# An attention and mixture-of-experts kernel: expert choice in eight operations a slot, three experts measured during attention, and scaling on ScalarE

## The chip, the cores and the metric

The kernel runs on one core of a Trainium2 chip. The metric is the time of one execution in microseconds on the device, as the median of several runs; smaller is better. One more execution was taken with the hardware profiler, and every row below comes from it. The engines are named as in the profile: PE is the matrix engine (PEld its weight loads), DVE is VectorE, ACT is ScalarE, POOL is GpSimd, SP is SyncE, which issues most of the DMAs.

## The reference

Attention over 8 batches and 8 heads of 576 tokens with 64 features, in which scores that lie more than `tau` below the row's maximum are dropped; its output, rearranged to 4608 rows of 512, goes through a mixture of 8 experts of which each row takes one. Everything is float32.

```python
scores = scale * np.matmul(q, k.transpose(0, 1, 3, 2))
thresh = np.max(scores, axis=-1, keepdims=True) - tau
scores = np.where(scores >= thresh, scores, -1000000000.0)
...softmax, then out = attn @ v
x = attn_out.transpose(0, 2, 1, 3).reshape(4608, 512)
logits = x @ w_gate                       # 512 x 8
e_idx = np.argmax(logits, axis=1)
gate_w = softmax(logits)[row, e_idx]
eom = sigmoid(x @ w_output_gate)
for e in range(8):
    mask = e_idx == e
    h = np.maximum(x[mask] @ w1[e], 0.0)  # 512 x 1024
    out[mask] = gate_w[mask, None] * eom[mask, e, None] * (h @ w2[e])
```

How many rows each expert gets is known only when the kernel runs.

## The kernel before

**Attention** takes about half of the span. It runs in 16 blocks of 9 steps, each block one pair of heads and batches, about 28 us long. PE computes scores, DVE reduces and thresholds them (L159, L189), ACT takes the exponential (L177), PE transposes and multiplies by the values, POOL normalises rows (L324, L325). As soon as rows of x are complete, they are routed: logits, the expert's number, and the place in the expert's list (`place`, L673), after which POOL's indirect DMA scatters the row into a table `xs` in DRAM, sorted by expert.

**Experts.** After attention come 13 units of work, numbered 0 to 12. Units 0 to 2 are early: they take the first 366, 256 and 424 rows of experts 0, 1 and 2, which are there before attention ends. Units 3 to 12 stand for the ten entries of `SLOTS`, taken in the order of `UNITS`; a slot is a number of rows, and which expert it serves is chosen at run time. A unit gathers its rows (`xg`, or `xgn` where it has 256), scales each row to a power of two (`even`, L928), transposes it and splits it in two fp16 halves xh and xl (`prep`), and then goes through 8 columns f: `first(f)` multiplies by 128 hidden features in 12 matmuls (xh, xl with w1h, w1l; L1260), ACT takes the relu and its high half (hr L1262, hh L969), DVE the low half (hl L975), and `second` follows two columns later (L1282 to L1285). Outputs `yo` are scaled by row (L956 on ACT, L958 on DVE) and scattered by POOL (L959).

**Weights** come in chunks of two columns, four chunks an expert, and are split in fp16 halves too: the high ones on ACT (w1h, w2h: L971), the low ones on DVE (w1l, w2l: L977). Before an expert's split its largest weight must be known: `measure` reduces each chunk (L874 on DVE, L875 on ACT), `peak` joins four chunks (L885, L886), `top` is a PE transpose of the result (L891) with a reduction and a diagonal behind it (L896, L897), and `spread` a PE matmul (L903) from which `powers` makes the scale. `SCALE` gives for a unit the column of peak, top and spread. PE takes its instructions in order, so the transpose of `top` stands in the row of matmuls and waits there for DVE.

Experts 0 and 1 (`FIRST = 2`) are measured during attention, in steps of blocks 1, 2, 3, 4, 6, 8, 12 and 15; all others in the expert stage, four columns or more after their load (`weigh`). Weights and rows of a unit can only be loaded once its slot has an expert (`known`).

**Choice.** `choose` fills the ten slots one after the other on DVE, on rows of 8 numbers, in 11 operations a slot; `aside` advances it between columns. For each slot it takes the expert with the most rows left whose remainder is not over the slot, and subtracts. `finish` then totals what is left over, in `sums` and `table` (on rows of up to 352 numbers), for a last loop (`rest`) which runs a whole extra unit for each leftover piece; `total` is the number of its passes.

Two order rules matter for the change. In the loop over columns (`run`) each column issues its matmuls first, then what else belongs to it, and each engine takes its own instructions in that order. And buffers: `egn` holds one gathered 256-row unit, and `eraw1`, the raw weights' second ring, is opened before the pools `ew1` to `ew3` of split weights.

Of the kernel before, what the change touches and what calls it, by code (L numbers as in the profile page):

```python
# [17 lines left out]
P = 128  # L18
# [412 lines left out]
class Router:  # L431
    SLOTS = (420, 396, 512, 504, 496, 256, 256, 256, 256, 256)
# [255 lines left out]

    def choose(self):
        V, E, row, dummy = self.nc.vector, self.E, self.row, self.dummy  # L690
        key, cand, mx, cm, got = row(E, "key"), row(E, "cand"), row(1, "mx"), row(1, "cm"), row(2, "got")
        st = self.st = self.sm.tile([1, 4, E], F32, name="st")
        pick = self.sm.tile([1, 2, E], F32, name="pick")
        V.tensor_tensor(st[:, 0], self.cnt[0:1], self.first[0:1], op=ALU.subtract)
# [53 lines left out]
    def sums(self, c, n):  # L748
        V = self.nc.vector
        V.memset(c[:, 0:1], 0.0)  # L750
        for e in range(self.E):
            V.tensor_tensor(c[:, e + 1 : e + 2], c[:, e : e + 1], n[:, e : e + 1], op=ALU.add)
            if e % 3 == 2:
                yield "vector"

    def table(self, sm, tag, out, c, size, first):
        V, E, NS = self.nc.vector, self.E, out.shape[2]
# [11 lines left out]
        V.tensor_tensor(ina, ina, inb, op=ALU.mult)  # L769
        yield "vector"  # L770
        V.tensor_scalar(v1, c[:, 0:E], -float(size), -dummy, op0=ALU.mult, op1=ALU.add)
        V.tensor_tensor(v1, v1, first, op=ALU.add)
        V.tensor_tensor(inb, ina, be(v1), op=ALU.mult)
        yield "vector"
        V.tensor_reduce(slf[:, 1], inb, axis=AX.X, op=ALU.add)
        V.tensor_reduce(slf[:, 2], ina, axis=AX.X, op=ALU.add)
        yield "vector"
        V.tensor_tensor(inb, ina, be(self.asc[0:1]), op=ALU.mult)
        V.tensor_reduce(slf[:, 0], inb, axis=AX.X, op=ALU.add)
        V.tensor_tensor(slf[:, 2], slf[:, 2], sid, op=ALU.mult)  # L780
        yield "vector"
        V.tensor_scalar(slf[:, 2], slf[:, 2], float(size), dummy, op0=ALU.mult, op1=ALU.add)
        V.tensor_tensor(slf[:, 1], slf[:, 1], slf[:, 2], op=ALU.add)
        V.tensor_copy(out, slf[:, 0:2])


class Experts:
    RINGS, NW, YB = (4, 4), 4, 4
    UNITS = (0, 6, 2, 7, 3, 8, 1, 5, 9, 4)
    TURN = (2,)  # L790
    FIRST = 2
    LOOK = 4
    SCALE = {2: (2, 4, 5), 3: (0, 1, 2), 4: (0, 1, 4)}

    def __init__(self, ctx, tc, rt, ident, w1, w2, out):
# [10 lines left out]
        self.gp, self.gn = [self.pool("eg", 1)], self.pool("egn", 1)  # L806
# [9 lines left out]
    def open(self):  # L816
# [17 lines left out]
        self.wp += [top(f"ew{i}", 1) for i in range(1, self.NW)]  # L834
# [81 lines left out]
    def even(self, xg):  # L916
# [72 lines left out]
    def begin(self):  # L989
# [9 lines left out]
        self.lines = [([n for n, t in enumerate(tiles) if t > 2], 2), ([n for n, t in enumerate(tiles) if t == 2], 1)]  # L999
        self.at, self.since, self.wide, self.pieces = {2: 1, 1: 1}, {1: -self.LOOK}, 0, []  # L1000
# [15 lines left out]
    def gather_next(self, i, f):  # L1016
        rt = self.rt
        passed = i + (f > 6)
        for line, room in self.lines:
            while self.at[room] < len(line):  # L1020
                k = self.at[room]
# [5 lines left out]
                self.at[room] += 1  # L1027
# [3 lines left out]
    def level(self, i, k):  # L1031
        for n in sorted(self.since):
            if self.column - self.since[n] >= self.LOOK or n == i + 1 and k >= -4:
# [81 lines left out]
    def run(self):  # L1115
# [4 lines left out]
        for i in range(nun):  # L1120
            b, final = self.unit(i), i == nun - 1
            late = i == rt.early - 1
            for f in range(8):
# [10 lines left out]
                if len(back) > 2:  # L1134
# [17 lines left out]
                rt.aside(2 if i else 1 if rt.tables else 4)  # L1152
# [32 lines left out]
class Base:  # L1185
# [24 lines left out]
    def even(self):  # L1210
        self.down, pieces = self.ex.even(self.xg[:, 0 : self.nt])
# [126 lines left out]
class Turned(Pair):  # L1338
# [148 lines left out]
def build(tc, qkv, tau, wg, w1, w2, out, shape):  # L1487
    nc = tc.nc
    with ExitStack() as ctx:
# [6 lines left out]
        with tc.manual_schedule(engines=ENGINES):  # L1496
            with ExitStack() as actx:
# [6 lines left out]
                load, size = ((0, 4), (0, 7), (1, 4), (1, 7), (2, 4), (4, 4), (4, 7), (6, 4)), (1, 2, 3, 4, 6, 8, 12, 15)  # L1504
# [24 lines left out]
                def second():  # L1529
# [4 lines left out]
                    ex.unit(0).key()  # L1534

                def first():
# [3 lines left out]
                    ws[2]()  # L1540
                    ws[3]()
# [58 lines left out]
```

## Time and profile before

| | us |
|---|---|
| median of 3 runs | 917.07 |
| the 3 runs | 915.4, 917.07, 917.15 |
| profiled execution | 915.95 |
| its span in the trace | 914.2 |
| attention, with its tail | 0 to about 472 |
| experts | about 462 to 915 |

The two stages overlap by some ten microseconds. The share of an engine's busy time is a mean over both; what a change in one stage is worth is read from that stage. In the views by window, PEclk is the clock that PE was granted: 1.00 is 2.4 GHz and 0.50 is 1.2 GHz.

### The profile page before, as it was taken

To read this page: it belongs to the slowest core of one execution; us is meant where nothing else is said; L and a number is where in the kernel's file an instruction comes from. 1 tells how busy PE (TensorE), PEld (TensorE's weight loads), DVE (VectorE), ACT (ScalarE), POOL (GpSimd) and SP (SyncE) were. 2 spreads that over 40 slices of the span, in tenths; PEclk is the share of its full clock that TensorE was granted. 3 is DMA by queue.
4 is the path that set the end of the run, shared out by engine and by line. 5 is a ranking of instruction groups with operands and counts; after the bars stand their busy time and mean duration, and the time that the engine had idled before them with its cause. 6 is when DMAs were issued, how large, how long until landed. Compare 5 with 4: busy or idle time off the path is not lost. (4 is left out here: it accounts for less than half of the span.)

```text
span 914.2 us, 22624 instructions
## 1 busy us (share of the span) xinstructions
PE 875.4 (96%) x8369; PEld 534.8 (59%) x8369; DVE 795.8 (87%) x1941; ACT 708.8 (78%) x1367; POOL 389.9 (43%) x660
## 2 busy tenths in 40 slices
PE   8999999999999999999988689899999999999996
PEld 4666666666666666666644444456546546566643
DVE  7999999999999999999977999988977877878731
ACT  6999999999989989898875665567857757867731
POOL 4465655757857678578735601021103103102101
PEclk9999999999999999999999999999999999999999
DMA  6499633143421234213259857445645636642001
GB/s 215 160 294 316 196 118 126 48 132 97 135 84 45 85 96 137 85 44 124 82 159 303 240 182 251 141 131 176 208 138 194 219 117 207 184 151 93 24 22 46
DMA packets 73810, 132.73 MB, mean 145 GB/s; under 512 B 6664, under 2 KB 35592, under 8 KB 73697
## 3 DMA queue, kind: packets, MB, share of 16 engines
q1 hardware_dynamic: 67153, 111.10, 38.8%
q0 software_dynamic: 6544, 20.16, 5.8%
q8 instruction: 67, 1.10, 0.5%
q14 instruction: 46, 0.38, 0.1%
HBM read 99.46 MB, written 32.74 MB: 145 GB/s over the span
## 5 line engine op out<-in xcount | busy, mean ns | idle before, releaser
L177 ACT ACTIVATE p<-s,mn 128x576 f32<-128x576 f32 x288 | 215.4, 796 | 22.6 <-DVE s L159 20.4
L189 DVE SCALAR_TENSOR_TENSOR p<-s,thr,p 128x576 f32<-128x576 f32 x288 | 225.9, 821 | 0.7 <-ACT p L177 0.3
L159 DVE TENSOR_SCALAR_CACHE_REDUCE s<-ps 128x576 f32<-128x576 f32 x288 | 206.2, 751 | 13.7 <-PE ps L145 11.1
L959 POOL DMA_INDIRECT out_dram<-yo,kid x39 | 49.7, 1274 | 330.9 <-DVE yo L958 234.7
L145 PE MATMUL ps<-qk 64*128 64x288 f32 (+1 forms) x1280 | 181.1, 418 | 0.0
L166 POOL TENSOR_SCALAR thr<-mn,tau_sb 128x2 f32<-128x2 f32 x144 | 103.3, 718 | 129.7 <-DVE s L159 125.8
L1260 PE MATMUL ph<-xh,w1l 128*128 128x256 f16 (+7 forms) x412 | 130.7, 319 | 1.9 <-DVE w1l L977 1.9
L1260 PE MATMUL ph<-xh,w1h 128*128 128x256 f16 (+7 forms) x412 | 131.6, 320 | 0.7 <-ACT w1h L971 0.7
L1260 PE MATMUL ph<-xl,w1h 128*128 128x256 f16 (+7 forms) x412 | 129.5, 319 | 2.4 <-DVE xl L975 2.4
L145 PEld LDWEIGHTS ps<-qk 64*128 64x128 f32 (+1 forms) x1280 | 107.2, 177 | 17.5 <-DVE s L159 2.5
L1262 ACT ACTIVATE hr<-ph 128x256 f32<-128x256 f32 (+7 forms) x103 | 48.0, 466 | 89.3 <-PE ph L1260 82.2
L1260 PEld LDWEIGHTS <-w1h 128*128 128x128 f16 x832 | 80.7, 99 | 56.9 <-issue 5.2
L258 PE MATMUL pr<-PTb,vld 128*64 128x320 f32 (+1 forms) x640 | 107.2, 447 | 0.0
L975 DVE TENSOR_TENSOR hl<-hr,hh 128x256 f16<-128x256 f32 (+7 forms) x103 | 54.3, 527 | 59.7 <-ACT hh L969 56.8
L244 PE MATMUL pt<-ident,p 64*128 64x64 f32 x2288 | 95.6, 223 | 1.5 <-ACT PTb L250 1.1
L258 PE MATMUL pa<-PTa,vld 128*64 128x256 f32 (+1 forms) x640 | 84.6, 391 | 0.3 <-ACT PTb L218 0.3
L244 PEld LDWEIGHTS pt<-ident,p 64*128 64x128 f32 x2288 | 82.9, 139 | 2.5 <-ACT PTb L250 1.4
L1282 PE MATMUL py<-w2h,hh 128*128 128x512 f16 (+3 forms) x213 | 82.0, 385 | 0.6 <-ACT yo L956 0.6
L1283 PE MATMUL py<-w2l,hh 128*128 128x512 f16 (+3 forms) x213 | 81.7, 384 | 0.0
L247 ACT COPY PTa<-pt 128x1024 f32<-128x1024 f32 x64 | 67.1, 1048 | 0.2 <-PE pt L244 0.2
L324 POOL TENSOR_TENSOR rows<-xl,rinv 128x256 f32<-128x256 f32 x64 | 62.1, 971 | 11.3 <-ACT xl L369 11.0
L247 ACT COPY PTb<-pt 128x1024 f32<-128x1024 f32 x63 | 65.1, 1034 | 1.2 <-PE ps L145 1.1
(244 smaller groups left out, 1707.4 us busy)
## 6 DMA issues: line engine op xcount, KB each, us to landing
r<-in_moe_w_dram SPq DMA_DIRECT2D x112, 512.0 KB
qk<-in_qkv_dram SPq DMA_DIRECT2D x31, 608.0 KB
xs<-zrow SPq DMA_DIRECT2D x44, 257.0 KB
vld<-in_qkv_dram SPq DMA_DIRECT2D x32, 320.0 KB
xg<-xs SPq DMA_DIRECT2D x4, 771.0 KB
xgn<-xs SPq DMA_DIRECT2D x6, 514.0 KB
xg<-xs SPq DMA_DIRECT2D x3, 1028.0 KB
xg<-xs SPq DMA_DIRECT2D x6, 128.5 KB
```

The costliest lines, as they stand in the source:

```text
L145: nc.tensor.matmul(ps[a][rows, o : o + HS], q[pp, t * P : t * P + w], k[pp, k0 : k0 + HS], start=True, stop=True)
L159: nc.vector.tensor_scalar(s, ps[a][:, c0 : c0 + S], SC, None, op0=ALU.mult, op1=ALU.min, accum_out=mn[:, a : a + 1])
L166: self.router.gate = nc.gpsimd.tensor_scalar(thr, mn, self.tau, None, op0=ALU.add)
L177: self.nc.scalar.activation(e, ss[a], AF.Exp, bias=mn[:, a : a + 1], scale=-1.0)
L189: nc.vector.scalar_tensor_tensor(e, s, thr[:, a : a + 1], e, op0=ALU.is_le, op1=ALU.mult, accum_out=acc[:, a ^ (t > 1) : (a ^ (t > 1)) + 1])
L244: nc.tensor.transpose(pt[:, o : o + 64], p[hs[h], k0 : k0 + P], id_[hs[h], hs[h]])
L247: nc.scalar.copy(d, pt.rearrange("p (h b j) -> p b h j", h=2, j=64))
L258: one = lambda out, l, r, start, stop: nc.tensor.matmul(out, l, r, start=start, stop=stop, skip_group_check=True)
L324: nc.gpsimd.tensor_tensor(o, xl[:, a, 0:4, 0:D], ra[:, a, 0:4, None].broadcast_to([P, 4, D]), op=ALU.mult)
L1260: nc.tensor.matmul(ph, w[:, c, fs], x[:, c, 0:N], start=(i == 0), stop=(i == 11))
L1282: nc.tensor.matmul(Y, hh[:, ts], wh, start=(f == 0), stop=False)
L1283: nc.tensor.matmul(Y, hh[:, ts], wl, start=False, stop=False)
```

## The change

The diff has ten parts.

1. `SLOTS` is put in another order (the 396 goes from second to sixth place) and `UNITS` with it. Each unit keeps its number of rows, but unit 4 now takes slot 1, where before it took slot 6.
2. `choose` needs 8 operations a slot, with the tie broken by a fraction added once to the counts, and stops at two places a slot instead of three. `aside` runs two pieces a column until three slots are filled, and then one a column from unit 2 on.
3. `sums` and `table` go from DVE to POOL; the reductions over 8 numbers become three additions of halves (`halved`).
4. `FIRST = 3`: expert 2's four chunks are loaded and measured during attention. Measures now stand in blocks 1, 2, 3, 4, 5, 6, 8, 9, 10, 12, 13 and 15 (5, 9, 10 and 13 are new).
5. The row scaling of units 1 to 5 is done by ACT.
6. `SCALE` holds units 3 and 4 alone: peak in column 3, top in 4, spread in 5 for unit 3, and 2, 4, 5 for unit 4. `weigh` starts at unit 2 for unit 3's chunks.
7. `egn` gets two buffers, so that 256-row units are gathered two ahead.
8. The pool `ew1` is opened before `eraw1`.
9. At the start, unit 0's second(0) comes before first(2), the splits of chunk 0's w2 come earlier, and the last `place` matmul comes a column later.
10. `key` runs at the second half of `prep`.

```diff
-    SLOTS = (420, 396, 512, 504, 496, 256, 256, 256, 256, 256)
+    SLOTS = (420, 256, 512, 504, 496, 396, 256, 256, 256, 256)
...
     def choose(self):
...
+        V.tensor_scalar(part, self.desc[0:1], 1.0 / (4 * E), None, op0=ALU.mult)
+        V.tensor_tensor(st[:, 0], st[:, 0], part, op=ALU.add)
...
         for k, z in enumerate(self.SLOTS):
             yield
-            V.scalar_tensor_tensor(key, st[:, 1], float(read), st[:, 0], op0=ALU.is_ge, op1=ALU.mult)
-            V.tensor_reduce(mx, key, axis=AX.X, op=ALU.max)
-            V.scalar_tensor_tensor(cand, key, mx, self.desc[0:1], op0=ALU.is_equal, op1=ALU.mult)
-            V.tensor_reduce(cm, cand, axis=AX.X, op=ALU.max)
+            V.scalar_tensor_tensor(key[:, 0:E], st[:, 1], float(read), st[:, 0], op0=ALU.is_ge, op1=ALU.mult)
+            V.tensor_reduce(top, key, axis=AX.X, op=ALU.max)
+            V.tensor_scalar(cand, key[:, 0:E], top, None, op0=ALU.is_equal)
+            V.tensor_tensor(pick, st[:, 2:4], cand[:, None, :].broadcast_to([1, 2, E]), op=ALU.mult)
             yield
-            V.tensor_scalar(key, key, 0.0, None, op0=ALU.is_gt)
-            V.scalar_tensor_tensor(cand, cand, cm, key, op0=ALU.is_equal, op1=ALU.mult)
-            V.tensor_tensor(pick, st[:, 2:4], cand[:, None, :].broadcast_to([1, 2, E]), op=ALU.mult)
             V.tensor_reduce(got, pick, axis=AX.X, op=ALU.add)
-            yield
...
     def table(self, sm, tag, out, c, size, first):
-        V.tensor_tensor(ina, bsl(sid), be(c[:, 0:E]), op=ALU.is_ge)
-        V.tensor_tensor(inb, bsl(sid), be(c[:, 1:]), op=ALU.is_lt)
+        for t, edge, op in ((ina, c[:, 0:E], ALU.is_ge), (inb, c[:, 1:], ALU.is_lt)):
+            G.tensor_tensor(t, bsl(sid), be(edge), op=ALU.subtract)
+            G.tensor_scalar(t, t, 0.0, None, op0=op)
...
-    UNITS = (0, 6, 2, 7, 3, 8, 1, 5, 9, 4)
+    UNITS = (0, 1, 2, 6, 3, 7, 5, 8, 9, 4)
-    FIRST = 2
+    FIRST = 3
-    SCALE = {2: (2, 4, 5), 3: (0, 1, 2), 4: (0, 1, 4)}
+    SCALE = {3: (3, 4, 5), 4: (2, 4, 5)}
...
-        self.gp, self.gn = [self.pool("eg", 1)], self.pool("egn", 1)
+        self.gp, self.gn = [self.pool("eg", 1)], self.pool("egn", 2)
...
+        self.wp.append(top("ew1", 1))
         self.raw.append(top("eraw1", self.RINGS[1]))
...
         def scale(a, b):
             for t in range(a, b):
-                V.tensor_scalar(xg[:, t, 0:DM], xg[:, t, 0:DM], up[:, t : t + 1], None, op0=ALU.mult)
+                if other:
+                    self.nc.scalar.activation(xg[:, t, 0:DM], xg[:, t, 0:DM], AF.Copy, scale=up[:, t : t + 1])
+                else:
+                    V.tensor_scalar(xg[:, t, 0:DM], xg[:, t, 0:DM], up[:, t : t + 1], None, op0=ALU.mult)
...
     def look(self, i, f):
-            if age >= self.LOOK:
+            n = self.fresh[0][0] // 4
+            if age >= self.LOOK and (i > 1 or n > 3) and (n == i + 1 or self.column % 2 == 0):
                 self.weigh()
...
     def run(self):
-                if len(back) > 2:
+                if len(back) > (1 if i == 0 and f == 1 else 2):
...
                 if rt.pending is not None:
+                    if rt.ripe:
+                        rt.place(self.ps_x.tile([P, 512], F32, name="px")[:, 0:144])()
                     rt.ripe = True
-                    rt.place(self.ps_x.tile([P, 512], F32, name="px")[:, 0:144])()
...
-                rt.aside(2 if i else 1 if rt.tables else 4)
+                rt.aside(2 if len(rt.tables) < 3 else int(i > 1))
...
-                load, size = ((0, 4), (0, 7), (1, 4), (1, 7), (2, 4), (4, 4), (4, 7), (6, 4)), (1, 2, 3, 4, 6, 8, 12, 15)
+                size = 1, 2, 3, 4, 5, 6, 8, 9, 10, 12, 13, 15
+                load = (0, 4), (0, 7), (1, 4), (1, 7), (2, 4), (2, 7), (4, 4), (4, 7), (5, 4), (6, 4), (8, 4), (9, 4)
```

On DVE, before, in unit 1, this is the stretch that ends in the peak of unit 2 (r_... are raw weights, st, key and cand are `choose`'s, hl and w1l belong to the columns):

```order
L977 SCALAR_TENSOR_TENSOR w2l<-r_8574,upe,w2h 128x1024
L874 TENSOR_REDUCE mx<-r_8819 128x1
L711 TENSOR_SCALAR picks<-got 1x1
L712 CAST picks<-got 1x1
L713 SCALAR_TENSOR_TENSOR st<-cand,st 1x24
L701 SCALAR_TENSOR_TENSOR key<-st 1x8
L702 TENSOR_REDUCE mx<-key 1x1
L703 SCALAR_TENSOR_TENSOR cand<-key,mx,desc 1x8
L704 TENSOR_REDUCE cm<-cand 1x1
L975 TENSOR_TENSOR hl<-hr,hh 128x256
L977 SCALAR_TENSOR_TENSOR w1l<-r_8668,upe,w1h 128x1024
L874 TENSOR_REDUCE mx<-r_8849 128x1
```

The rows after these are the peak, L885 and L886. The same columns of unit 1 in the changed kernel have neither a measure nor a step of the choice between the halves (w2l is L987 here, hl L985):

```order
L987 SCALAR_TENSOR_TENSOR w2l<-r_8611,upe,w2h 128x1024
L985 TENSOR_TENSOR hl<-hr,hh 128x256
L987 SCALAR_TENSOR_TENSOR w1l<-r_8687,upe,w1h 128x1024
L985 TENSOR_TENSOR hl<-hr,hh 128x256
L987 SCALAR_TENSOR_TENSOR w2l<-r_8688,upe,w2h 128x1024
L985 TENSOR_TENSOR hl<-hr,hh 128x256
L987 SCALAR_TENSOR_TENSOR w1l<-r_8707,upe,w1h 128x1024
```

Measures and choice have moved to unit 2, on the same engine. There the peak of unit 3 (L892, L893) stands one column ahead of the reduction that follows its transpose (L903):

```order
L985 TENSOR_TENSOR hl<-hr,hh 128x424
L881 TENSOR_REDUCE mx<-r_9144 128x1
L892 TENSOR_REDUCE red<-mx 128x2
L893 TENSOR_SCALAR red<-red 128x2
L712 SCALAR_TENSOR_TENSOR key<-st 1x8
L713 TENSOR_REDUCE top<-key 1x1
L714 TENSOR_SCALAR cand<-key,top 1x8
L715 TENSOR_TENSOR pick<-st,cand 1x16
L985 TENSOR_TENSOR hl<-hr,hh 128x424
L903 TENSOR_REDUCE most<-px 2x1
```

By `SCALE`, unit 3's peak closes column 3 and its transpose follows the matmuls of column 4; in the kernel before the peak of unit 2 closed column 2 of unit 1, two columns ahead, and that of unit 3 column 0 of unit 2, one column ahead.

On ACT, before, these are the rows at the start of the expert stage, from unit 0's first relu (h0r) to its second (hr):

```order
L1262 ACTIVATE h0r<-ps 128x366
L969 CAST h0h<-h0r 128x366
L971 ACTIVATE w2h<-r_1425,upe 128x1024
L369 COPY xl<-pa 128x400
L369 COPY xl<-pr 128x400
L971 ACTIVATE w1h<-r_2421,upe 128x1024
L971 ACTIVATE w2h<-r_2422,upe 128x1024
L971 ACTIVATE w1h<-r_2597,upe 128x1024
L1262 ACTIVATE hr<-ph 128x366
```

In the changed kernel they read:

```order
L981 ACTIVATE w2h<-r_2948,upe 128x1024
L277 COPY X_223<-pa 128x320
...
L1274 ACTIVATE h0r<-ps 128x366
L979 CAST h0h<-h0r 128x366
L369 COPY xl<-pa 128x400
L369 COPY xl<-pr 128x400
L981 ACTIVATE w1h<-r_3460,upe 128x1024
L981 ACTIVATE w2h<-r_3461,upe 128x1024
L981 ACTIVATE w1h<-r_4471,upe 128x1024
L1274 ACTIVATE hr<-ph 128x366
```

Chunk 0's w2h has moved ahead of h0r. Three splits still stand ahead of hr: those of chunk 1 and the first of chunk 2.

## Rows read from the trace of the kernel before

**Rows 1.** The page's first part: busy time, share of the span, instructions.
```profile
PE 875.4 (96%) x8369; PEld 534.8 (59%) x8369; DVE 795.8 (87%) x1941; ACT 708.8 (78%) x1367; POOL 389.9 (43%) x660
```
**Rows 2.** PE's waits from 462 to 915: total us, times, longest.
```profile
PE px L891 <- DVE red L886: 7.6, 2, 4.5
PE px L891 <- DVE red L885: 6.0, 1, 6.0
PE px L673 <- DVE ohb L588: 3.1, 1, 3.1
PE ph L1260 <- DVE xl L975: 2.4, 2, 1.2
PE px L1236 <- issue: 2.0, 1, 2.0
PE ph L1260 <- DVE w1l L977: 1.9, 1, 1.9
PE py L1285 <- DVE hl L975: 0.8, 1, 0.8
PE ph L1260 <- ACT w1h L971: 0.7, 1, 0.7
```
**Rows 3.** Windows in which PE's clock was halved (columns in the first line).
```profile
core 0: us, PE busy (x) PEld busy (x) DVE busy (x) ACT busy (x) POOL busy (x), PEclk, DMA share, GB/s
...
475.70:478.40 2.70, 2.66 (x9) 1.34 (x10) 1.27 (x2) 2.46 (x3) 0.41 (x2) 0.50 1.04 375
524.50:529.60 5.10, 5.04 (x18) 2.64 (x19) 4.74 (x20) 0.00 (x0) 3.04 (x4) 0.50 1.04 313
550.20:553.50 3.30, 3.30 (x9) 1.31 (x10) 3.13 (x12) 0.34 (x1) 0.00 (x0) 0.50 0.94 343
591.60:594.40 2.80, 2.75 (x9) 1.28 (x10) 2.35 (x8) 0.00 (x0) 0.00 (x0) 0.50 0.54 182
833.40:836.80 3.40, 3.40 (x25) 2.29 (x22) 2.32 (x4) 2.28 (x4) 0.00 (x0) 0.50 0.03 7
```
**Rows 4.** The same view of units 1 to 3 and of the seven units behind.
```profile
500.00:592.00 92.00, 74.08 (x449) 41.30 (x448) 87.62 (x241) 57.60 (x104) 22.79 (x21) 0.94 0.65 201
592.00:820.00 228.00, 227.99 (x1430) 129.95 (x1428) 185.19 (x303) 161.81 (x267) 33.78 (x29) 0.99 0.53 174
```
**Rows 5.** DVE from 500 to 592 by line: count, busy, mean ns, idle before.
```profile
L874 DVE TENSOR_REDUCE mx<-r 128x1 f32<-128x1024 f32 x13 | 15.7, 1204 | 0.0
L928 DVE TENSOR_SCALAR xg<-xg,xup 128x512 f32<-128x512 f32 x10 | 4.4, 478 | 0.0
L707 DVE SCALAR_TENSOR_TENSOR cand<-cand,cm,key 1x8 f32<-1x8 f32 x9 | 1.9, 215 | 0.3
L768 DVE TENSOR_TENSOR inbs<-sid,ci 1x352 f32<-1x352 f32 x1 | 0.5, 506 | 0.0
```
**Rows 6.** ACT from 470 to 910 by line.
```profile
L956 ACT ACTIVATE yo<-py,ksc 128x512 f32<-128x512 f32 x11 | 7.4, 686 | 14.9 <-PE py L1285 14.9
```
**Rows 7.** ACT's timeline at the start: start, us, instruction, idle before.
```profile
475.94 1.15 ACT L971 ACTIVATE w2h<-r,upe 128x1024 f16<-128x1024 f32 x1 [2.69 <-POOL rows L325]
```
**Rows 8.** Windows of three attention blocks, columns as in rows 3.
```profile
31.00:59.00 28.00, 28.00 (x364) 18.34 (x366) 27.44 (x76) 26.64 (x57) 16.17 (x29) 1.00 0.77 232
143.00:171.80 28.80, 28.80 (x368) 18.93 (x367) 28.50 (x84) 26.27 (x57) 18.98 (x40) 1.00 0.29 97
285.40:313.40 28.00, 28.00 (x364) 18.33 (x362) 26.98 (x80) 25.58 (x55) 17.49 (x28) 1.00 0.22 69
```
**Rows 9.** POOL from 100 to 460 by line.
```profile
L324 POOL TENSOR_TENSOR rows<-xl,rinv 128x256 f32<-128x256 f32 x50 | 48.8, 975 | 0.3
```
**Rows 10.** DVE's timeline at the end of attention, two rows of one line.
```profile
464.14 0.37 DVE L338 TENSOR_TENSOR LX<-LX,part 128x160 f32<-128x160 f32 x1
...
473.44 1.04 DVE L338 TENSOR_TENSOR LX<-LX,part 128x160 f32<-128x160 f32 x1
```
**Rows 11.** POOL's timeline at the second of these.
```profile
473.22 0.51 POOL L325 TENSOR_SCALAR rows<-xl,rinv 64x64 f32<-64x64 f32 x1
473.69 0.61 POOL L324 TENSOR_TENSOR rows<-xl,rinv 128x256 f32<-128x256 f32 x1
```

More of the change, by code (lines that the diff above doesn't have):

```diff
@@ L687, in open, with halved @@
         self.chosen = False
+    def halved(self, t, op):
+        n = self.E // 2
+        while n:
+            self.nc.gpsimd.tensor_tensor(t[..., 0:n], t[..., 0:n], t[..., n : 2 * n], op=op)
+            n //= 2
+        return t[..., 0]
     def choose(self):
         V, E, row, dummy = self.nc.vector, self.E, self.row, self.dummy
-        key, cand, mx, cm, got = row(E, "key"), row(E, "cand"), row(1, "mx"), row(1, "cm"), row(2, "got")
+        key, top, cand, got = row(E + 1, "key"), row(1, "top"), row(E, "cand"), row(2, "got")
         st = self.st = self.sm.tile([1, 4, E], F32, name="st")
         pick = self.sm.tile([1, 2, E], F32, name="pick")
+        part = row(E, "part")
+        V.memset(key[:, E:], 0.75)
         V.tensor_tensor(st[:, 0], self.cnt[0:1], self.first[0:1], op=ALU.subtract)
         V.tensor_scalar(st[:, 1], st[:, 0], float(P), float(self.SAFE), op0=ALU.add, op1=ALU.max)
+        V.tensor_scalar(part, self.desc[0:1], 1.0 / (4 * E), None, op0=ALU.mult)
+        V.tensor_tensor(st[:, 0], st[:, 0], part, op=ALU.add)
         V.tensor_scalar(st[:, 2], self.first[0:1], -1.0, dummy, op0=ALU.mult, op1=ALU.add)
@@ L756, in table @@
     def table(self, sm, tag, out, c, size, first):
-        V, E, NS = self.nc.vector, self.E, out.shape[2]
+        G, E, NS = self.nc.gpsimd, self.E, out.shape[2]
         sh = [1, NS, E]
@@ L766, in table @@
         dummy = float(E * self.CAP)
[L767 to L769 removed]
+        for t, edge, op in ((ina, c[:, 0:E], ALU.is_ge), (inb, c[:, 1:], ALU.is_lt)):
+            G.tensor_tensor(t, bsl(sid), be(edge), op=ALU.subtract)
+            G.tensor_scalar(t, t, 0.0, None, op0=op)
+        G.tensor_tensor(ina, ina, inb, op=ALU.mult)
         yield "vector"
[L771 to L773 removed]
+        G.tensor_scalar(v1, c[:, 0:E], -float(size), -dummy, op0=ALU.mult, op1=ALU.add)
+        G.tensor_tensor(v1, v1, first, op=ALU.add)
+        G.tensor_tensor(inb, ina, be(v1), op=ALU.mult)
+        G.tensor_copy(slf[:, 1], self.halved(inb, ALU.add))
         yield "vector"
[L775 to L776 removed]
+        G.tensor_tensor(inb, ina, be(self.asc[0:1]), op=ALU.mult)
+        G.tensor_copy(slf[:, 0], self.halved(inb, ALU.add))
         yield "vector"
[L778 to L784, printed above, removed]
+        G.tensor_tensor(slf[:, 2], self.halved(ina, ALU.add), sid, op=ALU.mult)
+        G.tensor_scalar(slf[:, 2], slf[:, 2], float(size), dummy, op0=ALU.mult, op1=ALU.add)
+        G.tensor_tensor(slf[:, 1], slf[:, 1], slf[:, 2], op=ALU.add)
+        G.tensor_copy(out, slf[:, 0:2])
 class Experts:
     RINGS, NW, YB = (4, 4), 4, 4
[L789 removed]
+    UNITS = (0, 1, 2, 6, 3, 7, 5, 8, 9, 4)
     TURN = (2,)
[L791 removed]
+    FIRST = 3
     LOOK = 4
[L793 removed]
+    SCALE = {3: (3, 4, 5), 4: (2, 4, 5)}
     def __init__(self, ctx, tc, rt, ident, w1, w2, out):
@@ L833, in open @@
         self.load_next()
-        self.wp += [top(f"ew{i}", 1) for i in range(1, self.NW)]
+        self.wp += [top(f"ew{i}", 1) for i in range(2, self.NW)]
     def load(self, e, g, gate=None, k=0):
@@ L914, in spread, with even @@
         return out
-    def even(self, xg):
+    def even(self, xg, other=False):
         V, n, DM = self.nc.vector, xg.shape[1], self.rt.DM
@@ L998, in begin @@
         tiles = [-(-(rt.base[n] if n < rt.early else rt.SLOTS[self.UNITS[n - rt.early]]) // P) for n in range(len(make))]
-        self.lines = [([n for n, t in enumerate(tiles) if t > 2], 2), ([n for n, t in enumerate(tiles) if t == 2], 1)]
-        self.at, self.since, self.wide, self.pieces = {2: 1, 1: 1}, {1: -self.LOOK}, 0, []
+        self.lines = [([n for n, t in enumerate(tiles) if t > 2], 2), ([n for n, t in enumerate(tiles) if t == 2], 2)]
+        self.at, self.since, self.wide, self.pieces = [1, 1], {1: -self.LOOK}, 0, []
         self.first_raws, self.column, self.fresh, self.mx, self.diag = [], 0, [], {}, None
@@ L1018, in gather_next @@
         passed = i + (f > 6)
-        for line, room in self.lines:
-            while self.at[room] < len(line):
-                k = self.at[room]
+        for c, (line, room) in enumerate(self.lines):
+            while self.at[c] < len(line):
+                k = self.at[c]
                 if k >= room and line[k - room] > passed:
@@ L1032, in level @@
         for n in sorted(self.since):
-            if self.column - self.since[n] >= self.LOOK or n == i + 1 and k >= -4:
+            if self.column - self.since[n] >= self.LOOK and (n < i + 3 or i > 4) or n == i + 1 and k >= -4:
                 del self.since[n]
@@ L1210, in even @@
     def even(self):
-        self.down, pieces = self.ex.even(self.xg[:, 0 : self.nt])
+        self.down, pieces = self.ex.even(self.xg[:, 0 : self.nt], 0 < self.i < 6)
         return pieces
@@ L1219, in prep @@
         ex, nc, rt, nt = self.ex, self.nc, self.ex.rt, self.nt
+        if k == 1 and later is None:
+            self.key()
         if k == 0:
-            if later is None:
-                self.key()
             n = 512 if ex.units[0] is not self else nt * P
@@ L1348, in prep @@
         ex, nc, xg, m = self.ex, self.nc, self.xg, self.nt - 1
+        if k == 1:
+            self.key()
         if k == 0:
-            self.key()
             self.xh, self.xl = (ex.xp.tile([P, 4, 512], F16, name=n) for n in ("xh", "xl"))
@@ L1534, in second @@
                     ex.unit(0).key()
+                    ws[2]()
+                    ws[3]()
                 def first():
```

10 lines of the change are left out of this document (4 added, 6 removed).

## The prediction

> **What bounds the kernel now.** I read the page's busy shares first, then PE's waits in the expert stage, then windows of that stage, then the lines of the engine PE waited for. PE is busy for 96% of the span [rows 1], so the change can only gain where PE stands still, where its clock is down, or where a block of attention gets shorter. The reader is to see in PE's waits that nearly everything it lost behind attention was waiting for DVE: the eight largest waits sum to 7.6 + 6.0 + 3.1 + 2.4 + 2.0 + 1.9 + 0.8 + 0.7 = 24.5 us, 21.8 of it for DVE [rows 2]. Two single waits for the peak's `red`, 6.0 in unit 1 and the 4.5 in the row of 7.6, are the longest; the other part of that row is 3.1, in unit 3.
>
> The windows show a second loss. In five short stretches PE worked at half clock, and each begins shortly after one of these waits. PE was busy there for 2.66 + 5.04 + 3.30 + 2.75 + 3.40 = 17.15 us [rows 3]; at full clock it would have been half, so 8.6 us went that way. Waits and clock give 24.5 + 8.6 = 33.1 us that a change here could win at most.
>
> The windows by stage say why: from 500 to 592, units 1 to 3, DVE was busy for 87.6 of 92.0 us and PE for 74.1, while in the next 228 us PE was busy for all but 0.01 us with DVE at 185.2 [rows 4]. So DVE bounds the first 92 us of units and PE the rest. Only what takes work off DVE in those 92 us counts.
>
> **The change, part by part.**
>
> *DVE from 500 to 592.* Four measures of expert 2 leave it: 4 x 1.20 = 4.8 us [rows 5]. The row scalings go to ACT: ten of 0.48 on `xg` and two like them on `xgn`, 5.7 us [rows 5]. The choice loses three operations of about 0.2 us (0.215 is the row of one of them) in each of nine slots: 27 x 0.2 = 5.4 us [rows 5]. The table's five or so operations of 352 numbers at 0.51 us, 2.5 us, go to POOL [rows 5]. The reductions and powers behind one peak and transpose, some six operations at 0.2 us by the same row, 1.2 us. Together 19.6 us. DVE then has 87.6 - 19.6 = 68.0 us of work there against PE's 74.1, less the 5.6 us of half clock (half of 5.04 + 3.30 + 2.75): 68.5 us [rows 3, 4]. That is an even balance, not slack. But steps of the choice and measures of unit 4 can now go on beyond 592, where DVE has (228.0 - 185.2)/228 = 19% to spare [rows 4]. I therefore count the waits as gone, with a remainder.
>
> *Unit 1.* Unit 2's peak and transpose are no longer there, as the order of DVE's rows shows. The 6.0 goes whole, and the half clock of 5.04 behind it, worth 2.5.
>
> *Units 2 and 3.* Two transposes remain. Unit 4's has its peak two columns ahead, and I count no wait. Unit 3's has one column between, and behind its peak stand a step of the choice (four operations) and one hl; the measure of the last chunk is just ahead of the peak. One column of PE is about 4.6 us in a 424-row unit by my estimate: 228 us in seven units of eight columns are 4.1 us [rows 4], for units that are on average smaller. Ahead of `red` in that column are hl, w1l or w2l and a measure, together some 3 to 4 us. So between 0 and 4.5 of that wait stays; I take 1.5, a third, as the choice ahead of it is shorter. With it stays some 0.9 of half clock. The waits for xl, 2.4 in two places, fall with DVE's load; I leave 0.6.
>
> *The start.* The wait of 3.1 for `ohb` is a matmul of `place`, which now follows a whole column later, behind six or more us of matmuls; it goes. The waits for w1l and w1h, 1.9 + 0.7 [rows 2], are of chunk 1, whose splits ACT and DVE took only once buffers were free: ACT stood 2.69 us for POOL's rows ahead of a w2h [rows 7]. The pools' new order moves that wait to the first split of chunk 2, and this stands in ACT's queue ahead of the second relu hr, for which PE's next `second` waits. So the stall is moved by a chunk and PE has more to do before it meets it: between 0 and 2.69 are left; I take 1.2.
>
> *The gather.* The 2.0 "issue" wait near 830 was for a unit's rows, loaded one ahead because `egn` had one buffer. With two, the rows come some eleven columns earlier; the wait and the half clock of 3.40 us behind it (1.7) go [rows 2, 3].
>
> *ACT.* It takes 16 scalings, of about 0.69 us by the nearest row, the scaled `yo` of the same shape [rows 6]: 11 us, of which about 8 fall from 500 to 592, where ACT was busy for 57.6 of 92.0 [rows 4]. That is hidden; without the cover it would be at most those 8 us.
>
> *POOL.* Some 40 table operations, most on rows of 352 numbers or less. The nearest row, a 128x256 multiplication on POOL, is 0.98 us [rows 9], the same table on DVE 0.51 [rows 5]; by these it is 20 to 40 us, in pieces, on an engine that had 69 us free from 500 to 592 [rows 4]. Nothing on PE's path reads the table before the last loop, so I count nothing. What can be queued behind are the scatters of `yo`, one piece of some 3 to 4 us each.
>
> *Attention.* Four measures more, 1.2 us of DVE each. In the three windows, blocks took 28.0 us with a measure (DVE 27.4), 28.8 with routing and none (DVE 28.5), and 28.0 with neither (DVE 27.0) [rows 8]. Blocks 5, 9 and 13 are of the second kind, where DVE is the bound and the 1.2 shows nearly whole; I take 1.1, 1.1 and 0.9. In block 10, of the third kind, 27.0 + 1.2 stands against 28.0: 0.3. Sum +3.4, between 0 (the neighbours' slack takes it) and 4 x 1.2 = 4.8. Four more megabytes of loads move while the DMA engines are at 22% to 29% in such blocks [rows 8]; I count nothing.
>
> *Sum.* 33.1 - (1.5 + 0.9 + 0.6 + 1.2 = 4.2) = 28.9 won, 3.4 lost: 25.5 net. From 915.95, the profiled execution, that is 890.4; the median shown lies 1.1 above this execution, so I predict 891 us.
>
> **A port that DVE and POOL share.** At the end of attention one and the same DVE addition with two operands in SBUF took 0.37 us alone and 1.04 while POOL went through its own row work [rows 10, 11]. The Trainium skill, "SBUF — State Buffer", section "Who interferes with whom", says that a VectorE operation with two SBUF inputs and a GpSimd operation that reads SBUF use one pair of ports, which the first of them holds for its whole instruction. By that rule the table on POOL would not be free, and the two rows agree with it. As a rival it is priced below from the rows alone.
>
> **Rivals.**
>
> *DVE is late again at both transposes.* The balance of 68.0 to 68.5 speaks for it: DVE has the same measures and nine slots of choice to do, now in units 2 and 3. Then 4.5 + 3.1 of waits stay in place of my 1.5, and the half clock of 3.30 and 2.75 (3.0) in place of my 0.9: 6.1 + 2.1 = 8.2 us more, 899. Against it: the choice no longer has a deadline in these units other than the slots' own loads.
>
> *POOL holds DVE back.* Each of 40 table operations could make one DVE operation such as hl, w1l or w2l longer by 1.04 - 0.37 = 0.67 us [rows 10]: 27 us. It falls in units 3 and 4, two times 33 us (228 over seven units), where DVE has 19% free, 12 us. Between 0 and 15 us come out on PE; half of it is 7.5, with a half clock of 1.7 as behind another wait: 900.
>
> *Waits were not for DVE's load.* If they were for weights arriving from DRAM (1.04 DMA share in two of the slow-clock windows [rows 3]), DVE's relief buys nothing, and attention costs its 3.4 or nothing: 914 to 919. Against it: PE's waits name `red` and DVE had no idle time ahead of the measures [rows 5].
>
> *Slower: one leftover token.* The new order of slots and the tie-break change which expert gets which slot. If after ten slots a single row of any expert is left over, the last loop runs one pass, loads a whole expert's weights and computes a unit by itself: some 33 us, 228 over seven [rows 4], nothing beside it. The time is then 891 + 33 = 924. It decides from the first such row on. Counted from the reference's inputs, the experts have 253, 240, 253, 491, 670, 499, 508 and 648 rows left after the early units, and the slots of either order cover them; in the new one the scarcest leaves three rows. Small differences in the logits would have to move more rows than that.
>
> *Better than stated.* No remainder at the start and at unit 3's transpose, attention at half its cost: 891 - 4.2 - 1.7 = 885, to 882 if the shorter DVE queue also shortens a block's tail.
>
> **How the numbers follow.** The forecast, 885 to 897 by its own unknowns (remainder 0 to 9, attention 0 to 4.8): 0.58. DVE late again, 899: 0.17. The port, 900: 0.10. Better, 882 to 885: 0.07. No change, 914 to 919: 0.04. Slower, 924: 0.04. Range 882 to 904: it leaves out the last two and some of the tails. A difference under 0.2%, 1.8 us, is what a measurement of this kernel can't tell from no change; by the cases faster has 0.93, the same 0.03 and slower 0.04.
>
> **What would show it.** Right: no wait of PE for `red` over 2 us, at most one stretch of half clock up to 600, DVE under 80% in unit 1, blocks 5, 9 and 13 of attention about 1 us longer, no wait for rows near 810. Wrong: a wait for `red` of over 3 us in unit 2 or 3 (late again); DVE's hl or w1l at more than 1.5 times their length while POOL is on the table (port); PE waits as before with DVE idle ahead of them (loads); a pass of the last loop behind the units (slower). My own weakest step is the balance of DVE in units 2 and 3, where 0.5 us decides by its sum and the pieces' order by its waits.

## The result, and the profile after

The changed kernel took 892.11 us, the median of four runs (890.94 to 892.45), against 916.67 for the kernel before in the same series: a ratio of 0.9732, 95% interval 0.9715 to 0.9749. In a second series, five runs each on another occasion, it was 0.9723 (0.9705 to 0.9741). The forecast was 891, range 882 to 904. The profiled execution took 890.94 and spans 889.2 us, 25.0 less than before.

In the first part of the page PE is now busy for 98% instead of 96% [rows 1]. DVE's total fell by only 18.5 us, POOL's rose by 22.5.

```profile
PE 869.6 (98%) x8367; PEld 532.7 (60%) x8367; DVE 777.3 (87%) x1869; ACT 718.0 (81%) x1383; POOL 412.4 (46%) x693
```

Most of the gain is in units 1 to 3. The next two fences show the same 24 columns in both kernels, from unit 0's last relu to unit 3's last: first before, then after. The columns are those of [rows 3].

```profile
501.90:621.60 119.70, 101.78 (x615) 56.92 (x614) 111.82 (x286) 73.86 (x129) 26.13 (x24) 0.94 0.59 185
```

```profile
500.30:600.10 99.80, 95.71 (x604) 54.75 (x602) 84.02 (x196) 76.78 (x134) 30.01 (x30) 0.98 0.68 226
```

These units take 19.9 us less, and DVE does 27.8 us less in them. Part of that work was only moved: behind them DVE has 214.1 us to do (600.1 to 889.2) where it had 207.3 (621.6 to 914.2). PE's mean clock in the 24 columns rose from 0.94 to 0.98. Behind them PE was already fully busy, and the time left to win was the gather near 830.

PE's waits from 462 to the end, in the form of [rows 2], show what is left of the 24.5 us listed there (the largest four):

```profile
PE py L1394 <- DVE yo L968: 3.1, 1, 3.1
PE px L898 <- DVE red L893: 1.9, 2, 1.2
PE pr L312 <- ACT PTb L218: 0.8, 1, 0.8
PE px L898 <- DVE key L712: 0.7, 1, 0.7
```

The 6.0 and the 7.6 for `red`, the 3.1 for `ohb`, the waits for w1l and w1h and the 2.0 for rows are gone. In their place stands one that was not there: 3.1 us for a `yo` of unit 1 in unit 2, because PE's next `py` goes into the buffer that this `yo` reads. One stretch of half clock follows it (there were five, [rows 3]):

```profile
537.70:541.10 3.40, 3.40 (x12) 1.44 (x10) 3.23 (x10) 0.93 (x2) 1.85 (x3) 0.50 1.06 355
```

DVE's timeline names its origin. The columns are start, us, instruction, and in brackets the idle time before it with what ended it.

```profile
530.48 1.22 DVE L881 TENSOR_REDUCE mx<-r 128x1 f32<-128x1024 f32 x1
533.51 1.22 DVE L928 TENSOR_REDUCE ax<-xg 128x2 f32<-128x1024 f32 x1 [1.82 <-DMA xg<-xs]
...
535.04 0.58 DVE L985 TENSOR_TENSOR hl<-hr,hh 128x424 f16<-128x424 f32 x1
535.55 0.73 DVE L968 TENSOR_SCALAR yo<-py,ksc 128x512 f32<-128x512 f32 x1
```

DVE stood idle for 1.82 us, because the row maxima of unit 3 were next in its order and the rows had not arrived. `hl` and the `yo` that PE needs stood behind it: between DVE falling idle at 531.7 and the end of `yo` at 536.3 lie the 1.82, the row maxima, four operations of the choice (0.4), `hl` and `yo` itself. From 503 to 530 the DMA engines had no time to spare, where before they were at 0.86.

```profile
503.00:530.00 27.00, 26.71 (x189) 16.51 (x187) 22.39 (x46) 20.76 (x39) 18.94 (x16) 1.00 1.01 340
```

That full engines made the rows late is likely and not shown, because DVE also came sooner. Of these lines the first is of the changed kernel, the others of the kernel before: the issue of the same gather on SP in both, DVE's row maxima of unit 3, and a window in which the DMA engines (0.02) were all but still:

```profile
521.47 1.81 SPq L1338 DMA_DIRECT2D xg<-xs  x3
536.75 3.43 SPq L1326 DMA_DIRECT2D xg<-xs  x4
549.99 1.22 DVE L921 TENSOR_REDUCE ax<-xg 128x2 f32<-128x1024 f32 x1
547.00:548.00 1.00, 0.00 (x0) 0.00 (x0) 0.86 (x9) 0.02 (x1) 0.00 (x0) 1.00 0.02 8
```

DVE now came to the rows 10.2 us after their issue (531.7) and got them after 12.0 (533.5). Before, it came after 13.2, and the engines had been all but still from 547 on, some 10 us after the issue. So the rows took some 2 us longer and DVE asked some 3 us sooner; no run separates the two.

Attention paid as forecast in place, and less in size. Blocks 5, 9 and 13, which had 28.8, 28.8 and 28.6 us, take 29.5, 29.6 and 28.9, and block 10 28.1 instead of 28.0. That is +1.9 for the four. The first of these blocks, as in [rows 8]:

```profile
143.00:172.50 29.50, 29.29 (x368) 18.75 (x364) 29.18 (x85) 27.25 (x59) 18.97 (x40) 1.00 0.39 130
```

### The profile page after: what moved, and what is told of

Read it like the earlier page. It is cut to its first block, busy times and chain, and to the rows that moved or that the text cites. A ratio compares the mean times of both kernels' runs of the same rounds, so it can differ in the third digit from the quotient of the medians.

```text
span 889.2 us, 22622 instructions
## 1 busy us (share of the span) xinstructions
PE 869.6 (98%) x8367; PEld 532.7 (60%) x8367; DVE 777.3 (87%) x1869; ACT 718.0 (81%) x1383; POOL 412.4 (46%) x693
## 5 line engine op out<-in xcount | busy, mean ns | idle before, releaser
L159 DVE TENSOR_SCALAR_CACHE_REDUCE s<-ps 128x576 f32<-128x576 f32 x288 | 206.3, 751 | 13.2 <-PE ps L145 11.2
L145 PE MATMUL ps<-qk 64*128 64x288 f32 (+1 forms) x1280 | 183.4, 419 | 0.4 <-DVE s L159 0.4
L985 DVE TENSOR_TENSOR hl<-hr,hh 128x256 f16<-128x256 f32 (+7 forms) x103 | 55.5, 539 | 54.5 <-ACT hh L979 52.6
```

The lines of the kernel that those rows point to most:

```text
L145: nc.tensor.matmul(ps[a][rows, o : o + HS], q[pp, t * P : t * P + w], k[pp, k0 : k0 + HS], start=True, stop=True)
L159: nc.vector.tensor_scalar(s, ps[a][:, c0 : c0 + S], SC, None, op0=ALU.mult, op1=ALU.min, accum_out=mn[:, a : a + 1])
```

## The experiments

All are edits of the changed kernel. The kernel before ran in each series and its median moved between 914.5 and 917.2 us, so ratios to it are compared and not times. The changed kernel lies at 0.9728, the mean of its two series; 0.0011 of ratio is 1 us, and a difference of two ratios is uncertain by about 2 us.

**Measuring expert 2 in the expert stage again.**

```diff
-    FIRST = 3
+    FIRST = 2
...
-    SCALE = {3: (3, 4, 5), 4: (2, 4, 5)}
+    SCALE = {2: (2, 4, 5), 3: (3, 4, 5), 4: (2, 4, 5)}
...
-            if age >= self.LOOK and (i > 1 or n > 3) and (n == i + 1 or self.column % 2 == 0):
+            if age >= self.LOOK and (i > 1 or n > 3 or n == 2) and (n == i + 1 or self.column % 2 == 0):
...
-                size = 1, 2, 3, 4, 5, 6, 8, 9, 10, 12, 13, 15
-                load = (0, 4), (0, 7), (1, 4), (1, 7), (2, 4), (2, 7), (4, 4), (4, 7), (5, 4), (6, 4), (8, 4), (9, 4)
+                size = 1, 2, 3, 4, 6, 8, 12, 15
+                load = (0, 4), (0, 7), (1, 4), (1, 7), (2, 4), (4, 4), (4, 7), (6, 4)
```

> The changed kernel with expert 2 measured in the expert stage again (FIRST = 2, its peak, transpose and spread in columns 2, 4 and 5 of unit 1). Theory, DVE bounds units 1 to 3: a wait for red in unit 1 comes back (it was 6.0 us, with 2.5 of half clock behind it), and DVE gets 4.8 + 1.2 us there; attention gets some 2 us shorter. Sum +3 to +9 on 892.1: 895 to 901. Rival, the waits were for loads: attention's 2 us are won and nothing is lost, 889 to 891.

893.63 us, ratio 0.9772 (0.9759 to 0.9786): +4.0. PE's waits show the stall of unit 1 again, 5.6 against 6.0 before, although choice, scaling and table are still off DVE:

```profile
PE px L898 <- DVE red L893: 7.5, 3, 5.6
```

The stall in unit 1 is that of the measures, with the peak and transpose that go with them. In the traces the last matmul of attention's values starts at 466.6 instead of 469.5, so attention gave back 2.9 us, some 2 of it in the four blocks, and the measures cost some 7 in the expert stage.

**The start as before.**

```diff
-        self.wp.append(top("ew1", 1))
...
-                if len(back) > (1 if i == 0 and f == 1 else 2):
+                if len(back) > 2:
...
-                    if rt.ripe:
-                        rt.place(self.ps_x.tile([P, 512], F32, name="px")[:, 0:144])()
                     rt.ripe = True
+                    rt.place(self.ps_x.tile([P, 512], F32, name="px")[:, 0:144])()
...
                     ex.unit(0).key()
-                    ws[2]()
-                    ws[3]()
...
                     ex.unit(0).first(0)
+                    ws[2]()
+                    ws[3]()
```

> The changed kernel with the start as before: ew1 opened behind eraw1, second(0) behind first(2), w2's splits of chunk 0 behind h0r, place one column earlier. Theory: the waits of 3.1 (ohb), 1.9 (w1l) and 0.7 (w1h) and the half clock of 1.3 come back: +7, 899. Rival, the stalls at the start only moved on to a later wait: within 1 us of 892.

895.52 us, ratio 0.9796 (0.9782 to 0.9809): +6.2. The three waits are back in full:

```profile
PE px L673 <- DVE ohb L588: 3.6, 1, 3.6
...
PE ph L1270 <- DVE w1l L986: 1.9, 1, 1.9
...
PE ph L1270 <- ACT w1h L980: 0.7, 1, 0.7
```

Together they are 6.2 us. The half clock that the theory counted with them did not come back:

```profile
475.00:485.00 10.00, 5.03 (x30) 2.78 (x31) 8.35 (x18) 7.40 (x11) 2.91 (x4) 1.00 1.03 360
```

**The start's order alone as before, ew1 still opened first.** The diff is that of the run above without the line of `ew1`.

> The changed kernel with the start's order as before (second(0), w2's splits, place) but with ew1 opened first. Theory: the 3.6 us wait for ohb comes back and the 2.6 for w1h and w1l do not: +3.6 to +5, ratio 0.976 to 0.978. Rival, with the splits early the place is reached later and the wait shrinks: 0 to +2.

892.65 us, ratio 0.9755 (0.9742 to 0.9768): +2.5. Here both my theory and its rival fail on the waits. Those for chunk 1's weights came back with the order alone, and the one for `ohb` did not:

```profile
PE ph L1271 <- DVE w1l L987: 1.9, 1, 1.9
...
PE ph L1271 <- ACT w1h L981: 0.7, 1, 0.7
PE px L673 <- DVE ohb L588: 0.4, 1, 0.4
```

So the pools' order by itself does not take the waits for w1h and w1l away; the new order of the start has to be there. Which of its three edits does it (second(0), the splits of w2, `place`) is not shown, since they were undone together. With the pools as before as well, the 3.6 for `ohb` follows. The old order of the pools under the new start was not run.

**One buffer for 256-row units.**

```diff
-        self.gp, self.gn = [self.pool("eg", 1)], self.pool("egn", 2)
+        self.gp, self.gn = [self.pool("eg", 1)], self.pool("egn", 1)
...
-        self.lines = [([n for n, t in enumerate(tiles) if t > 2], 2), ([n for n, t in enumerate(tiles) if t == 2], 2)]
+        self.lines = [([n for n, t in enumerate(tiles) if t > 2], 2), ([n for n, t in enumerate(tiles) if t == 2], 1)]
```

> The changed kernel with one buffer for gathered 256-row units, so that they are gathered one ahead. Theory: the 2.0 us wait for rows ahead of unit 11 and its half clock of 1.7 come back, +3.7: 895.8. Rival, the rows are there in time now because SP's queue is shorter: 892.

892.42 us, ratio 0.9759 (0.9746 to 0.9773): +2.8. The wait returns to the tenth, and the half clock behind it:

```profile
PE px L1248 <- issue: 2.0, 1, 2.0
```

```profile
812.00:815.40 3.40, 3.40 (x27) 2.54 (x26) 2.07 (x4) 2.12 (x3) 0.00 (x0) 0.51 0.02 5
```

**Row scaling on DVE.**

```diff
-        self.down, pieces = self.ex.even(self.xg[:, 0 : self.nt], 0 < self.i < 6)
+        self.down, pieces = self.ex.even(self.xg[:, 0 : self.nt])
```

> The changed kernel with units 1 to 5 scaling their rows on DVE again: 16 operations of 0.48 us, some 12 of them in units 1 to 3. Theory, DVE and PE are evenly balanced there: +2 to +6, 894 to 898, with longer waits for red or hl. Rival, DVE has room since the measures left: within 1 us of 892.

892.87 us, ratio 0.9761 (0.9743 to 0.978): +3.0, with runs from 890.83 to 895.14. The transpose of unit 3 waits 3.2 us for `red` where it waited 0.7; the other two of the three waits below are those of units 4 and 5, as in the changed kernel.

```profile
PE px L898 <- DVE red L893: 5.1, 3, 3.2
```

**Eleven operations a slot.** `choose` of the kernel before, put back whole.

> The changed kernel with the choice in eleven operations a slot, in three pieces, as before. Theory, DVE and PE are evenly balanced in units 2 and 3: 27 operations of 0.2 us are 5.4 us, of which +1 to +4 show, in the transposes of units 3 and 4. Rival, DVE has room in the later units and the choice spreads into it: within 0.5 us of the changed kernel.

890.98 us, ratio 0.9713 (0.9699 to 0.9728): -1.4, no difference that can be told from zero. The waits at the transposes did grow, from 0.7 to 2.2 at unit 3's, but the one for `yo` fell from 3.1 to 1.8, and nothing was at half clock:

```profile
PE px L898 <- DVE key L708: 2.2, 1, 2.2
PE py L1394 <- DVE yo L968: 1.8, 1, 1.8
PE px L898 <- DVE red L893: 1.5, 1, 1.5
```

The waits of the theory came, and a shorter wait for `yo` and the missing half clock made up for them. The time is nearer the rival: by itself the shorter choice buys nothing that can be measured here, to within some 2 us.

**The table on DVE.** `sums` and `table` of the kernel before, put back whole.

> The changed kernel with sums and table on DVE as before. By the forecast's sum, DVE gets 2.5 us back in a place where it has room by now: 0 to +1, ratio 0.9723 to 0.974. Rival, POOL's work on the table held DVE back at the port that they share: -1 to -4, ratio 0.968 to 0.971, with hl never over 0.7 us.

890.96 us, ratio 0.9735 (0.9722 to 0.9748): +0.6, no difference that can be told from zero. The rival's gain did not come. But in the changed kernel's trace the contention itself is seen: five `hl` of 256 columns took 0.47, 0.55, 0.55, 0.61 and 1.05 us, each beside an operation of the table, against about 0.42 for the others of their shape. This is the longest, with the operation of POOL that it overlaps:

```profile
604.35 1.05 DVE L985 TENSOR_TENSOR hl<-hr,hh 128x256 f16<-128x256 f32 x1
```

```profile
603.32 1.79 POOL L775 TENSOR_TENSOR inbs<-sid,ci 1x352 f32<-1x352 f32 x1
```

With the table on DVE no `hl` of 256 columns took over 0.44 us, and none of any shape over 0.69. It happens, to a few instructions, in units where DVE has time.

**All four reliefs of DVE undone at once.** The edits of the runs on measuring, scaling, choice and table together.

> The changed kernel with all four reliefs of DVE undone at once: expert 2 measured in the expert stage, rows scaled on DVE, the table on DVE, eleven operations a slot. The order of slots, the start and the two gather buffers stay. Theory, DVE and PE balance evenly in units 1 to 3, so that one relief undone finds room and all together do not: more than the sum of the single ones (some 6 us), +9 to +14, ratio to the kernel before 0.983 to 0.988. Rival, the prices simply add, +5 to +7: ratio 0.978 to 0.981.

900.02 us, ratio 0.984 (0.9827 to 0.9853): +10.3. The four singly sum to 4.0 + 3.0 - 1.4 + 0.6 = 6.2. The time lies in the range of the theory, with waits of 6.1 and 3.0 for `red` and two for `hl`, 2.9 together:

```profile
PE px L899 <- DVE red L894: 9.1, 2, 6.1
PE py L1298 <- DVE hl L986: 2.9, 2, 2.1
```

But four differences, each uncertain by 2 us, can be 4 off together: that the reliefs need each other is likely from these waits, and not settled by the times.

**Slots and units in the order of before.**

```diff
-    SLOTS = (420, 256, 512, 504, 496, 396, 256, 256, 256, 256)
+    SLOTS = (420, 396, 512, 504, 496, 256, 256, 256, 256, 256)
...
-    UNITS = (0, 1, 2, 6, 3, 7, 5, 8, 9, 4)
+    UNITS = (0, 6, 2, 7, 3, 8, 1, 5, 9, 4)
...
-                rt.aside(2 if len(rt.tables) < 3 else int(i > 1))
+                rt.aside(2 if i else 1 if rt.tables else 4)
```

> The changed kernel with the order of slots and units as before and the choice at two pieces a column throughout, so that unit 4 serves slot 6 again. Theory, the 3.1 us wait for red at unit 4's scale was DVE's load and is small now: 0 to +2, ratio 0.972 to 0.975. Rival, it was the late choice, since unit 4's weights can be loaded only then: +3 to +5, ratio 0.976 to 0.978, with a wait of 3 us or more for red in unit 3.

890.66 us, ratio 0.9736 (0.9722 to 0.9749): +0.7, no difference that can be told from zero. There is no wait of 3 us for `red` (the longest is 1.5); the rival is out. With DVE relieved it does not show in the time that unit 4's expert is chosen late. PE's longest wait is another one, for a `yo`, in unit 1:

```profile
PE py L1294 <- DVE yo L968: 3.8, 1, 3.8
```

**The changed kernel again, and two tries at what it still waits for.** The first edit puts the row maxima of units 3 and 4 later in DVE's order, the second also the transposes of units 5 and 6.

```diff
-            if self.column - self.since[n] >= self.LOOK and (n < i + 3 or i > 4) or n == i + 1 and k >= -4:
+            if self.column - self.since[n] >= (6 if n in (3, 4) else self.LOOK) and (n < i + 3 or i > 4) or n == i + 1 and k >= -4:
```

```diff
-    SCALE = {3: (3, 4, 5), 4: (2, 4, 5)}
+    SCALE = {3: (3, 4, 5), 4: (2, 4, 5), 5: (-2, 1, 2), 6: (-2, 1, 2)}
```

> The changed kernel, nothing edited, on the chip of the next three runs, so that they and the ones before can be set against it: ratio to the kernel before 0.973 as in its first timing (0.9715 to 0.9749).

> The changed kernel with the row maxima (ax) of units 3 and 4 put later in DVE's order: two columns for unit 4, one for unit 3. Theory: DVE stood 1.8 us for unit 3's rows from DRAM with hl and yo queued behind, and this made PE's 3.1 us wait for yo and the half clock of 1.7; they go, and the transpose of unit 3 waits up to 1 us longer: -3 to -5 on the changed kernel. Rival, DVE is simply behind there and the wait moves to the next hl or to red: within 1 us of the changed kernel.

> As the run with later row maxima, and besides the transposes of units 5 and 6 one column later (top in column 1, spread in 2). Theory: the waits of 1.2 and 0.7 for red there go too, -2 more. Rival, the later scale makes the split of unit 5's first chunk late and PE waits for w1h or w1l instead: 0 to +2.

In one series: 891.53 us for the changed kernel, 890.97 and 889.28 for the two. The ratios are 0.9723 (0.9705 to 0.9741), 0.9711 (0.9695 to 0.9727) and 0.9697 (0.9681 to 0.9712), so -1.1 and -2.4 us. The first can't be told from zero and lies outside its theory's -3 to -5. The waits that were aimed at are gone: with both edits neither `yo` nor `red` is in PE's list.

```profile
PE ph L1272 <- ACT xh L979: 2.5, 1, 2.5
PE ph L1272 <- DVE xl L985: 1.0, 1, 1.0
PE pr L312 <- ACT PTb L218: 0.8, 1, 0.8
PE px L1411 <- DVE down L887: 0.5, 1, 0.5
```

But a wait for `xh` leads the list, and less was won than forecast. It is not of these edits' making: the changed kernel, profiled again in this series, had it too, and not the wait for `yo`.

```profile
PE ph L1272 <- ACT xh L979: 2.7, 1, 2.7
PE px L898 <- DVE red L893: 1.9, 2, 1.2
PE px L898 <- DVE key L712: 1.2, 1, 1.2
```

The kernel with both edits is the fastest of all runs here. Its five runs (888.59 to 890.69) lie below all five of the changed kernel's (890.86 to 893.93); the intervals of the two ratios still overlap a little.

**What the runs account for.** All four reliefs of DVE, the start and the second buffer, undone, cost 10.3 + 6.2 + 2.8 = 19.3 us. The changed kernel lies 0.0272 of ratio, some 24.9 us, below the kernel before. The other 5.6 have no run of their own: parts 6 and 10 of the change were never undone by themselves, and such a sum of differences can be 3 to 4 us off.

## Why the prediction was right, step by step

- **The balance of DVE in units 1 to 3** was right in direction and too pessimistic. I had DVE and PE even, 68.0 against 68.5, in the 92 us to 592. In the 24 columns of units 1 to 3 it is no even balance: DVE is busy for 84.0 of 99.8 us and PE for 95.7. The 19.6 us that I had leaving DVE and the 27.8 that left can't be set side by side, since the second stretch is longer. The sum had a slip, too: the half clock from 591.6 to 594.4 lies behind the stretch that it was taken from, so PE's side was some 69.7; and 890.4 + 1.1 is 891.5 and not 891.
- **Unit 1**: the 6.0 and its half clock went, as stated. The run with measures back shows that they, with their peak and transpose, were the cause.
- **The transposes**: I left 1.5 for unit 3's and none for unit 4's; it was 0.7 and none in this trace. The waits of 1.2 and 0.7 for `red` in units 4 and 5 were not in the sum. DVE has 6.8 us more to do behind unit 3; that this made them is argued and not shown.
- **The start**: 1.2 us were to stay, none did. The price of the whole was near (5.7 of waits and 1.3 of clock, less the 1.2; 6.2 by the run, all of it waits), the mechanism in part not: I gave the waits for w1h and w1l to the pools' order, and the run with the start's order as before shows that the pools' order alone does not remove them.
- **The gather**: 3.7 forecast, 2.8 by the run with one buffer, with the wait and the half clock at the forecast sizes.
- **ACT and POOL**: nothing that the times show, as forecast, though PE waits 2.7 for ACT's `xh` in the second profile (last section). The table's place makes no difference to the time that can be told, and neither does the choice's length: by themselves two of the change's parts, and the order of slots with them, show nothing here.
- **Attention**: +3.4 forecast. It ends 2.5 us later in the trace, 1.9 of it in the four blocks and 0.6 already at the first step of the first block, which no edit explains. Block 13 took 0.3 where I put 0.9.
- **What failed** is the remainder in the expert stage. I wrote 4.2; the gaps of over 0.25 us behind attention's last matmuls and the half clock make 3.1 + 0.7 + 1.2 + 0.7 + 0.3 + 1.7 = 7.7, of which only the 0.7 stood where I had put some. The 4.8 of the new stall (3.1 and 1.7) came from DVE standing for unit 3's rows: I priced neither a transfer that is late nor a relieved DVE that comes to it sooner.

So the total of 25.5 against 25.0 in the traces is nearer than its parts, and that is partly luck. Attention was priced 0.9 too high, and the expert stage won 1.4 less than stated: 28.9 forecast, 27.5 measured. A remainder of 7.7 in place of 4.2 would have left only 25.4 of the 33.1. The other 2.1 were not in my list: 1.1 of them are two waits of the kernel before, below the eight of [rows 2], and 1.0 I can't place.

```profile
PE py L1282 <- ACT yo L956: 0.6, 1, 0.6
PE px L1358 <- DVE down L880: 0.5, 1, 0.5
```

Of the signs that I named for being right, one failed: DVE was to be under 80% in unit 1, and is busy for 22.06 of 25.60 us there, 86%. PE waited all the same for no measure in that unit.

```profile
500.30:525.90 25.60, 25.31 (x184) 16.11 (x182) 22.06 (x51) 19.39 (x38) 21.18 (x18) 1.00 0.97 315
```

The rivals: DVE late at both transposes fell (0.7 us and none), the loads were not what PE waited for before, and no pass of the last loop ran (PE has 8367 matmuls, two fewer than before). The port is real and did not decide. Its sign did appear, one `hl` at 2.5 times its length, and its time did not. The pair of rows that I gave for it was misread: the addition of 0.37 us, which I called alone, had a POOL operation beside it too.

```profile
464.02 0.45 POOL L325 TENSOR_SCALAR rows<-xl,rinv 64x64 f32<-64x64 f32 x1
```

A piece of the loads' rival did come true after the change: PE's longest wait now goes back to rows that had not landed.

## What to carry to other kernels

Count what a relieved engine frees, and then ask which instruction in its queue waits for a transfer: with DVE relieved the loads came closer together, the DMA engines went from 0.86 to full between 503 and 530, and the next stall was an instruction queued early for rows that had not landed. A stall of PE can be worth more than its row says: the 2.0 us wait for rows in the kernel before and the 3.1 for `yo` in the changed one were each followed by 3.40 us at half clock, 1.7 lost. Not each was: none followed the 3.6 for `ohb` in the run with the start as before. And undo the parts of a change one by one: here measuring, scaling, the start and the second buffer carry most of the gain, while the reworked choice, the table on POOL and the new order of slots show nothing by themselves.

## What was not expected of the hardware

In the second profile of the changed kernel, ACT stood still for 5.09 us ahead of an `xh`, though the transposes that this instruction reads had ended at 521.24. Its timeline shows no work and no engine that released it:

```profile
521.24 0.41 ACT L979 CAST hh<-hr 128x256 f16<-128x256 f32 x1
526.74 0.96 ACT L979 CAST xh<-px 128x384 f16<-128x384 f32 x3 [5.09 <-remote]
```

```profile
520.70 0.54 PE L1371 MATMUL px<-ident,xg 64*128 64x64 f32 x12
```

In the half microsecond around the restart the DMA view lists a packet of an instruction queue between full data queues:

```profile
q0 software_dynamic: 29, 0.12, 57.8%
q1 hardware_dynamic: 38, 0.08, 39.9%
q14 instruction: 1, 0.01, 3.9%
```

The same place had idle times of 3.0, 4.4 and 5.3 us in three other traces (the changed kernel's first, and the two with later row maxima) and none over 1.4 us in the nine other traces of the changed kernel and its edits. Of these three, only the trace with both later edits has a packet of that queue just ahead of the restart (524.5 to 525.0, restart at 525.35); the other two have none in the two microseconds before it. The kernel before has an idle time of this kind in another place, 1.5 us of it after the transposes had ended (496.1), with the DMA engines at 0.65 and no such packet in the 3 us before:

```profile
497.62 1.07 ACT L969 CAST xh<-px 128x512 f16<-128x512 f32 x2 [3.10 <-remote]
```

That ACT waited for its own instructions while the DMA engines were full is a guess that fits two of the four traces. No run here tells it from another cause, and it stays open.
